# Layer scale on one core: held-back loads, 8-row first blocks, and stores released by a landing

## The chip, the cores and the metric

The kernel runs on one core of a Trainium2 chip. The metric is the device time in microseconds (us) of that core. It is a pure streaming job: two large inputs come in from device memory (HBM), one output of the same size goes out, and in between stand one multiplication and one addition for each element.

## The reference

```python
B, S, D = 1024, 16, 512
x: bfloat16 [B, S, D]
y: bfloat16 [B, S, D]
gamma: bfloat16 [D]

def reference(x, y, gamma):
    return x + gamma * y
```

Flattened, x and y have 16384 rows of 512 elements. The kernel gives each of the 128 partitions of on-chip memory (SBUF) 128 such rows. "A row" below means one row on every partition: 128 x 512 bf16 elements, 128 KB. x, y and the output have 128 of them each, so the DMA engines move 384 rows, 50.33 MB.

## The kernel before

Everything is laid out by a few tables at the head. `BLOCKS` cuts the 128 rows into blocks that are contiguous per partition in HBM; a DMA moves rows of one block, so a load of 64 rows moves 64 KB per partition in one packet. `PIECES` cuts the rows again for VectorE. `SP` lists the loads that SyncE issues, in order; `ACT` lists what ScalarE issues: gamma and the stores; `DVE` lists VectorE's multiplies ('m') and adds ('a') by piece.

```python
BLOCKS = [4, 64, 60]
PIECES = [4, 11, 53, 60]

SP = [
    ('y', 0, 4),
    ('y', 4, 68),
    ('x', 4, 68, 0),         # the last number: first slot in x_sb
    ('y', 68, 128),
    ('x', 68, 128, 11),
    ('x', 0, 4, 0),
]
ACT = [('g',), ('s', 4, 68), ('s', 68, 128), ('s', 0, 4)]

EARLY = (2, 0)               # SyncE's first two loads go before the start barrier

DVE = [('m', 0), ('m', 1), ('m', 2), ('a', 2), ('a', 1), ('m', 3), ('go',), ('a', 3), ('a', 0)]
```

y has its whole place in SBUF (128 slots of 1 KB per partition), and multiply and add work in place on it. x has 71 slots; its later blocks reuse the slots of the first block, so their loads wait until the adds that read those slots are done. Issuing, one list per engine (`_take` waits for a semaphore and takes its count off again):

```python
    def ring(eng, what, n_early):
        known, went = 0, False
        for k, w in enumerate(what):
            kind = w[0]
            need = frees(w) if kind == "x" else pieces_of(w[1], w[2]) + list(w[3:]) if kind == "s" else []
            need = max((order[c] + 1 for c in need), default=0)
            if kind == "s" and not went:
                _take(s_go, 1, eng)          # the first store waits for "go"
                went = True
            if need > known:
                eng.wait_ge(s_add, need)     # adds done so far
                known = need
            # ... dma_start of gamma, of an x load, of a y load, or of a store
```

gamma comes as one row, is spread over the 128 partitions by a matmul with a row of ones, and is cast to bf16:

```python
    nc.vector.memset(ones_row, 1.0).then_inc(s_ones, 1)
    _take(s_ones, 1, nc.tensor)
    _take(s_gamma, 16, nc.tensor)
    nc.tensor.matmul(gamma_ps, ones_row, gamma_row, start=True, stop=True).then_inc(s_ps, 1)
    _take(s_ps, 1, nc.vector)
    nc.vector.tensor_copy(out=gamma_sb, in_=gamma_ps).then_inc(s_dve, 1)
```

VectorE's list:

```python
    for kind, *args in DVE:
        if kind == "go":
            _take(s_dve, open_mults, nc.vector)   # all multiplies are done
            open_mults = 0
            nc.vector.sem_inc(s_go, 1)            # stores may start
            continue
        c = args[0]
        yt = y_sb[:, starts[c] : starts[c + 1], :]
        if kind == "m":
            need(y_loads, c)                      # waits for the y loads of this piece
            # ... yt = yt * gamma  (L166)
        else:
            need(x_loads, c)                      # waits for the x loads of this piece
            # ... yt = xt + yt     (L175)
```

Of the kernel before, what the change touches and what calls it, by code (L numbers as in the profile page):

```python
# [3 lines left out]

BLOCKS = [4, 64, 60]

PIECES = [4, 11, 53, 60]


SP = [
    ('y', 0, 4),
    ('y', 4, 68),
    ('x', 4, 68, 0),
    ('y', 68, 128),
    ('x', 68, 128, 11),
    ('x', 0, 4, 0),
]
ACT = [('g',), ('s', 4, 68), ('s', 68, 128), ('s', 0, 4)]  # L20

EARLY = (2, 0)

DVE = [('m', 0), ('m', 1), ('m', 2), ('a', 2), ('a', 1), ('m', 3), ('go',), ('a', 3), ('a', 0)]
MULT, ADD = mybir.AluOpType.mult, mybir.AluOpType.add


def _take(sem, n, eng):


    return eng.wait_ge(sem, n).then_inc(sem, -n)  # L31


def kernel(
    tc: tile.TileContext,
    x: bass.AP,
    y: bass.AP,
    gamma: bass.AP,
    out: bass.AP,
):  # L40

    nc = tc.nc
    P = nc.NUM_PARTITIONS
    tc.close()
    tc.compile()  # L47

    xf = x.flatten_outer_dims()
    yf = y.flatten_outer_dims()  # L50
    of = out.flatten_outer_dims()
    N, D = xf.shape
    rows = N // P
    n = len(PIECES)
    assert sum(PIECES) == rows
    starts = [sum(PIECES[:c]) for c in range(n + 1)]
    dt = xf.dtype
    edges = [sum(BLOCKS[:c]) for c in range(len(BLOCKS) + 1)]
    assert edges[-1] == rows

    def rows_of(t, a, b):

        c = max(c for c in range(len(BLOCKS)) if edges[c] <= a)
        assert b <= edges[c + 1]
        block = t[P * edges[c] : P * edges[c + 1]].rearrange("(p n) d -> p n d", p=P)
        return block[:, a - edges[c] : b - edges[c], :]

    gamma_row = nc.alloc_sbuf_tensor("gamma_row", [1, D], dt).ap()
    ones_row = nc.alloc_sbuf_tensor("ones_row", [1, P], dt).ap()
    gamma_sb = nc.alloc_sbuf_tensor("gamma_sb", [P, D], dt).ap()  # L70
    y_sb = nc.alloc_sbuf_tensor("y_sb", [P, rows, D], dt).ap()
    x_loads = [w for w in SP + ACT if w[0] == "x"]
    y_loads = [w for w in SP + ACT if w[0] == "y"]
    stores = [w for w in SP + ACT if w[0] == "s"]
    for loads in (x_loads, y_loads, stores):
        assert sum(w[2] - w[1] for w in loads) == rows
    x_rows = max(w[3] + w[2] - w[1] for w in x_loads)
    x_sb = nc.alloc_sbuf_tensor("x_sb", [P, x_rows, D], dt).ap()
    gamma_ps = nc.alloc_psum_tensor("gamma_ps", [P, D], mybir.dt.float32).ap()

    sem = nc.alloc_semaphore
    s_gamma, s_ones, s_ps, s_dve = sem("s_gamma"), sem("s_ones"), sem("s_ps"), sem("s_dve")
    s_load = {w: sem("s_" + "_".join(map(str, w[:2]))) for w in x_loads + y_loads}
    s_add, s_go, s_end, s_out = sem("s_add"), sem("s_go"), sem("s_end"), sem("s_out")
    added = [a for kind, *a in DVE if kind == "a"]
    order = {a[0]: k for k, a in enumerate(added)}

    def meets(a, b, c, d):
        return a < d and c < b

    def pieces_of(a, b):
        return [c for c in range(n) if meets(starts[c], starts[c + 1], a, b)]

    def x_at(row):
        return next(w[3] + row - w[1] for w in x_loads if w[1] <= row < w[2])

    def frees(w):

        c = set()
        for v in x_loads[: x_loads.index(w)]:  # L100
            lo, hi = max(v[3], w[3]), min(v[3] + v[2] - v[1], w[3] + w[2] - w[1])
            if lo < hi:
                c |= set(pieces_of(v[1] + lo - v[3], v[1] + hi - v[3]))
        return sorted(c)

    early = []

    def ring(eng, what, n_early):

        known, went = 0, False  # L110
        for k, w in enumerate(what):
            kind = w[0]
            need = frees(w) if kind == "x" else pieces_of(w[1], w[2]) + list(w[3:]) if kind == "s" else []
            need = max((order[c] + 1 for c in need), default=0)
            if kind == "s" and not went:
                _take(s_go, 1, eng)
                went = True
            if need > known:
                eng.wait_ge(s_add, need)
                known = need  # L120
            if kind == "g":
                i = eng.dma_start(out=gamma_row, in_=gamma.unsqueeze(0)).then_inc(s_gamma, 16)
            elif kind == "x":
                to = x_sb[:, w[3] : w[3] + w[2] - w[1], :]
                i = eng.dma_start(out=to, in_=rows_of(xf, w[1], w[2])).then_inc(s_load[w], 16)
            elif kind == "y":
                r = slice(w[1], w[2])
                i = eng.dma_start(out=y_sb[:, r, :], in_=rows_of(yf, w[1], w[2])).then_inc(s_load[w], 16)
            else:
                r = slice(w[1], w[2])  # L130
                i = eng.dma_start(out=rows_of(of, w[1], w[2]), in_=y_sb[:, r, :]).then_inc(s_out, 16)
            if k < n_early:
                early.append(i.ins)

    ring(nc.sync, SP, EARLY[0])
    ring(nc.scalar, ACT, EARLY[1])


    nc.vector.memset(ones_row, 1.0).then_inc(s_ones, 1)  # L139
    _take(s_ones, 1, nc.tensor)  # L140
    _take(s_gamma, 16, nc.tensor)
    nc.tensor.matmul(gamma_ps, ones_row, gamma_row, start=True, stop=True).then_inc(s_ps, 1)  # L142
    _take(s_ps, 1, nc.vector)
    nc.vector.tensor_copy(out=gamma_sb, in_=gamma_ps).then_inc(s_dve, 1)  # L144
    _take(s_dve, 1, nc.vector)

    landed, open_mults = set(), 0

    def need(loads, c):
        for w in loads:  # L150
            if w not in landed and meets(starts[c], starts[c + 1], w[1], w[2]):
                _take(s_load[w], 16, nc.vector)
                landed.add(w)

    for kind, *args in DVE:
        if kind == "go":
            _take(s_dve, open_mults, nc.vector)
            open_mults = 0
            nc.vector.sem_inc(s_go, 1)
            continue  # L160
        c = args[0]
        yt = y_sb[:, starts[c] : starts[c + 1], :]
        if kind == "m":
            need(y_loads, c)
            g = gamma_sb[:, None, :].to_broadcast([P, PIECES[c], D])
            nc.vector.tensor_tensor(out=yt, in0=yt, in1=g, op=MULT).then_inc(s_dve, 1)  # L166
            open_mults += 1
        else:
            need(x_loads, c)
            if open_mults:  # L170
                _take(s_dve, open_mults, nc.vector)
                open_mults = 0
            at = x_at(starts[c])
            xt = x_sb[:, at : at + PIECES[c], :]
            nc.vector.tensor_tensor(out=yt, in0=xt, in1=yt, op=ADD).then_inc(s_add, 1)  # L175


    nc.scalar.sem_inc(s_end, 1)
    _take(s_end, 1, nc.sync)
    _take(s_add, n, nc.sync)  # L180
    _take(s_out, 16 * len(stores), nc.sync)

    main = nc.main_func.blocks[0].instructions
    names = {i.name for i in early}
    for b in nc.main_func.blocks[1:]:
        for i in [i for i in b.instructions if i.name in names]:
            b.instructions.remove(i)
    for k, i in enumerate(early):
        main.insert(1 + k, i)
# [30 lines left out]
```

## Time and profile before

| what | before |
|---|---|
| device time, median of 3 runs | 120.48 us (120.41 to 120.82) |
| span of the profiled run (120.82 us) | 119.5 us |
| VectorE busy | 70.1 us (59%), 10 instructions |
| TensorE busy | 0.6 us (one matmul) |
| y rows 0 to 4: issued, landing | 0.0 us, 3.3 us later |
| first store issued | 76.98 us |
| first store (8 MB), issue to landing | 23.1 us |

How to read the profile: PE is TensorE, DVE is VectorE, POOL is GpSimd; SPq and ACTq are the sequencers of SyncE and ScalarE, which issue the DMAs. A line such as L166 is a line of the kernel. The span is cut into 40 slices, and each digit is the busy share of a slice in tenths. DMA is the mean busy share of the core's 16 DMA engines. A DMA queue is listed with its packets, its megabytes and the time that its packets took, as a share of 16 engines' span. A line of the timeline has the start, the time taken, the engine, the operation and its shapes; an "x2" joins two operations that follow each other. In brackets stands how long the engine had been idle before it.

### The profile page before, as it was taken

The numbers are of one execution on the slowest core, as the hardware profiler recorded it, in microseconds if no ns is written. First come the engines' busy times: TensorE is split into PE (matmuls) and PEld (weight loads), VectorE is DVE, ScalarE is ACT, GpSimd is POOL, SyncE is SP. The second block draws the span as 40 slices with busy tenths as digits, with TensorE's granted clock in tenths as the row PEclk, the third lists the DMA queues.
The fourth block names the chain that finished last, engine by engine and source line by source line (L and its number), as shares of the span: only waits on it lengthen the run. The fifth ranks groups of instructions, "written<-read, shape, count | busy, mean of one in ns | idle before, by whom it ended". The sixth has DMA issues, their size and how long they took to land. (4 is left out here: it accounts for less than half of the span.)

```text
span 119.5 us, 79 instructions
## 1 busy us (share of the span) xinstructions
PE 0.6 (0%) x1; PEld 0.1 (0%) x1; DVE 70.1 (59%) x10; POOL 0.2 (0%) x4
## 2 busy tenths in 40 slices
PE   0001000000000000000000000000000000000000
PEld 0000000000000000000000000000000000000000
DVE  0001400299999579999979999649999930000000
POOL 0000000000000000000000000000000000000000
DMA  9888998889888987987998998798998899899874
GB/s 527 351 351 351 483 570 351 351 351 702 351 351 351 639 370 329 617 370 329 535 432 350 411 555 350 329 527 351 592 439 373 351 557 432 350 473 494 350 337 167
DMA packets 1298, 50.33 MB, mean 421 GB/s; under 512 B 145, under 2 KB 146, under 8 KB 530
## 3 DMA queue, kind: packets, MB, share of 16 engines
q1 hardware_dynamic: 864, 33.55, 65.6%
q10 hardware_dynamic: 434, 16.78, 32.5%
HBM read 33.56 MB, written 16.78 MB: 421 GB/s over the span
## 5 line engine op out<-in xcount | busy, mean ns | idle before, releaser
L166 DVE TENSOR_TENSOR y_sb<-y_sb,gamma_sb 128x2048 bf16<-128x2048 bf16 (+3 forms) x4 | 34.7, 8690 | 10.5 <-DVEq L31 10.5
L175 DVE TENSOR_TENSOR y_sb<-x_sb,y_sb 128x27136 bf16<-128x27136 bf16 (+3 forms) x4 | 34.6, 8689 | 4.9 <-DVEq L31 4.9
L144 DVE CAST gamma_sb<-gamma_ps 128x512 bf16<-128x512 f32 x1 | 0.7, 692 | 9.3 <-DVEq L31 9.3
L139 DVE MEMSET ones_row<- 1x128 bf16 x1 | 0.2, 165 | 2.0 <-PEq L47 2.0
L142 PE MATMUL gamma_ps<-gamma_row,ones_row 1*128 1x512 bf16 x1 | 0.6, 577 | 10.7 <-PEq L31 10.7
L142 PEld LDWEIGHTS gamma_ps<-gamma_row,ones_row 1*128 1x128 bf16 x1 | 0.1, 99 | 10.7 <-issue 10.7
L204 POOL MEMSET const-bfloat16-1.0<- 128x1 bf16 x1 | 0.1, 102 | 0.0
L204 POOL MEMSET const-uint8-127<- 128x1 uint8 x1 | 0.1, 102 | 0.0
L204 POOL MEMSET const-float32-1.0<- 128x1 f32 x1 | 0.1, 99 | 0.0
L204 POOL MEMSET const-float32-0.0<- 128x1 f32 x1 | 0.1, 98 | 0.2 <-issue 0.2
## 6 DMA issues: line engine op xcount, KB each, us to landing
y_sb<-in_y_dram SPq DMA_DIRECT2D x1, 7680.0 KB, 58.1
x_sb<-in_x_dram SPq DMA_DIRECT2D x1, 7680.0 KB, 22.4
out_dram<-y_sb ACTq DMA_DIRECT2D x1, 7680.0 KB, 22.4
y_sb<-in_y_dram SPq DMA_DIRECT2D x1, 512.0 KB, 3.3
x_sb<-in_x_dram SPq DMA_DIRECT2D x1, 512.0 KB, 20.9
out_dram<-y_sb ACTq DMA_DIRECT2D x1, 512.0 KB, 22.7
y_sb<-in_y_dram SPq DMA_DIRECT2D x1, 22.5
x_sb<-in_x_dram SPq DMA_DIRECT2D x1, 40.4
```

Of the source, the lines that this page charges most:

```text
L139: nc.vector.memset(ones_row, 1.0).then_inc(s_ones, 1)
L142: nc.tensor.matmul(gamma_ps, ones_row, gamma_row, start=True, stop=True).then_inc(s_ps, 1)
L144: nc.vector.tensor_copy(out=gamma_sb, in_=gamma_ps).then_inc(s_dve, 1)
L166: nc.vector.tensor_tensor(out=yt, in0=yt, in1=g, op=MULT).then_inc(s_dve, 1)
L175: nc.vector.tensor_tensor(out=yt, in0=xt, in1=yt, op=ADD).then_inc(s_add, 1)
L204: nc = _bacc.Bacc("TRN2", target_bir_lowering=False, num_devices=1)
```

## The change

Three things change together.

- The blocks become 8, 60 and 60 rows in place of 4, 64 and 60, and VectorE's pieces 8, 15, 45 and 60 rows. x's 8 rows are its last load, and the last store has 8 rows. x now needs 75 slots.
- The third load (x), the fourth (y) and gamma are held back until y's first 8 rows have landed. TensorE waits for that landing and tells SyncE, ScalarE and VectorE by a semaphore each.
- The first store is no longer released by VectorE after the last multiply. TensorE waits until x's second block (rows 68 to 128) has landed, and then releases the stores and VectorE's last large add.

It is meant to keep the DMA queues short at the start, so that nothing goes beside the first rows, and to keep stores from running beside the last large load; x's 8 small rows are left in the queue to bridge the turn from loads to stores.

```diff
-BLOCKS = [4, 64, 60]
-PIECES = [4, 11, 53, 60]
+BLOCKS = [8, 60, 60]
+PIECES = [8, 15, 45, 60]

 SP = [
-    ('y', 0, 4),
-    ('y', 4, 68),
-    ('x', 4, 68, 0),
+    ('y', 0, 8),
+    ('y', 8, 68),
+    ('x', 8, 68, 0),
     ('y', 68, 128),
-    ('x', 68, 128, 11),
-    ('x', 0, 4, 0),
+    ('x', 68, 128, 15),
+    ('x', 0, 8, 0),
 ]
-ACT = [('g',), ('s', 4, 68), ('s', 68, 128), ('s', 0, 4)]
+ACT = [('g',), ('s', 8, 68), ('s', 68, 128), ('s', 0, 8)]

+HOLD = ('y', 0, 8)
+RELEASE = ('x', 68, 128, 15)
-DVE = [('m', 0), ('m', 1), ('m', 2), ('a', 2), ('a', 1), ('m', 3), ('go',), ('a', 3), ('a', 0)]
+DVE = [('m', 0), ('m', 1), ('m', 2), ('a', 2), ('a', 1), ('m', 3), ('a', 3), ('a', 0)]
 ... (semaphores s_held_sp, s_held_act, s_held_dve, s_rel)
         for k, w in enumerate(what):
             kind = w[0]
+            if k == n_early:
+                _take(s_held[eng], 1, eng)
 ...
     nc.vector.memset(ones_row, 1.0).then_inc(s_ones, 1)
+    _take(s_load[HOLD], 16, nc.tensor)
+    for s_one in s_held.values():
+        nc.tensor.sem_inc(s_one, 1)
     _take(s_ones, 1, nc.tensor)
     _take(s_gamma, 16, nc.tensor)
 ... (matmul and cast as before)
+    _take(s_load[RELEASE], 16, nc.tensor)
+    nc.tensor.sem_inc(s_go, 1)
+    nc.tensor.sem_inc(s_rel, 1)
 ... (VectorE's need())
-                _take(s_load[w], 16, nc.vector)
+                if w == RELEASE:
+                    _take(s_rel, 1, nc.vector)
+                elif w == HOLD:
+                    _take(s_held[nc.vector], 1, nc.vector)
+                else:
+                    _take(s_load[w], 16, nc.vector)
 ... (VectorE's list)
-        if kind == "go":
-            _take(s_dve, open_mults, nc.vector)
-            open_mults = 0
-            nc.vector.sem_inc(s_go, 1)
-            continue
```

## The prediction

> **What bounds the kernel now.** I read the page first (its slices, the DMA queues, the costliest groups), then VectorE's timeline, then tables of busy time by stage, then single packet records of the trace around the three places that the change touches: the start, the turn from loads to stores, and the end.
>
> The page's slices and its queue part come first:
>
> ```profile
> DVE  0001400299999579999979999649999930000000
> DMA  9888998889888987987998998798998899899874
> ...
> q1 hardware_dynamic: 864, 33.55, 65.6%
> q10 hardware_dynamic: 434, 16.78, 32.5%
> HBM read 33.56 MB, written 16.78 MB: 421 GB/s over the span
> ```
>
> The DMA engines are busy in every slice. The two queues' packets fill 65.6% + 32.5% = 98.1% of the 119.5 us, which is 117.2 us; so an average engine idles only 2.3 us, before its first packet and after its last. VectorE is busy for 59%. The loads are on q1 (SyncE's), the stores on q10 (ScalarE's).
>
> VectorE's timeline says what it waits for (start us, us, what; in brackets the idle time before):
>
> ```profile
> 12.36 1.23 DVE L166 TENSOR_TENSOR y_sb<-y_sb,gamma_sb 128x2048 bf16<-128x2048 bf16 x1 [0.26 <-DVEq L31]
> 23.06 17.29 DVE L166 TENSOR_TENSOR y_sb<-y_sb,gamma_sb 128x5632 bf16<-128x5632 bf16 x2 [9.48 <-DVEq L31]
> 42.52 17.29 DVE L175 TENSOR_TENSOR y_sb<-x_sb,y_sb 128x27136 bf16<-128x27136 bf16 x2 [2.16 <-DVEq L31]
> 60.55 16.16 DVE L166 TENSOR_TENSOR y_sb<-y_sb,gamma_sb 128x30720 bf16<-128x30720 bf16 x1 [0.74 <-DVEq L31]
> 79.41 17.30 DVE L175 TENSOR_TENSOR y_sb<-x_sb,y_sb 128x30720 bf16<-128x30720 bf16 x2 [2.70 <-DVEq L31]
> ```
>
> Every stage of VectorE starts when a load has landed and ends before the next one lands: it is 0.7 to 2.7 us ahead each time. Sixty rows cost it 16.16 us, the same rows cost the DMA 18.1 us (60 KB packets of 2.267 us, eight per engine and load). So VectorE sets no end; it only has to hand over the stores in time.
>
> The last view is busy time around the turn and at the end (in each row: stretch, its length, busy time of four engines, clock, DMA share, GB/s; a packet counts where it starts, so a share can pass 1):
>
> ```profile
> 77.70:80.41 2.71, 0.00 (x0) 0.00 (x0) 1.00 (x1) 0.00 (x0) 1.00 1.32 556
> 80.41:116.00 35.59, 0.00 (x0) 0.00 (x0) 16.30 (x2) 0.00 (x0) 1.00 0.99 429
> 116.00:119.50 3.50, 0.00 (x0) 0.00 (x0) 0.00 (x0) 0.00 (x0) 1.00 0.37 150
> ```
>
> From the first load to 116 us there is no hole. The packet records at the turn show why: VectorE's "go" at 76.7 us lets ScalarE issue the first store at 76.98; the fastest engine ends x's last 4 rows at 78.97 and starts its first store packet the same instant, the slowest does so at 80.41. At the end the 4 KB packets of the last store finish at 117.7 us on the fastest engine, at 118.5 on the last but one and at 119.1 on the last, whose completion is seen at 119.46. That last engine is late because one packet of x's rows 68 to 128, started at 59.71, took 3.30 us in place of 2.27.
>
> **What the Trainium skill says.** "DMA: Bandwidth & Descriptors", section "Issuing engines are not separate DMA queues": transfers issued by different engines run on the same 16 DMA engines. The trace agrees: the two queues' shares add up to 98.1%. The same page, section "Queues, rings and completion order", lets an engine go round-robin between its queues at packet boundaries. Here that is seen only in part: the slowest engine ended all eight packets of x's 4 rows before its first store packet at 80.41, though other engines were storing from 78.97. I therefore count on queued loads finishing first. "Perfetto Trace Analysis", section "DMA Instruction — HWDGE (DVE, Sync)": the reported time of a DMA instruction is its issue, and completion comes after a confirmed last write. The trace has 0.37 us for issuing the first store and 23.1 us to its landing. "VectorE: DVE Perf Modes", section "The perf-mode tier table", has bf16 tensor-tensor work at two elements a cycle, 1224 ns for 2048 elements; the trace has 1226 and 1220 ns.
>
> **The change part by part.**
>
> 1. Block sizes, 4/64/60 to 8/60/60. Bytes stay 384 rows of 128 KB. Per engine before: 24 packets of 64 KB at 2.418, 24 of 60 KB at 2.267 and 24 of 4 KB at 0.159 (medians of the trace): 58.03 + 54.41 + 3.82 = 116.26 us. After: 48 of 60 KB and 24 of 8 KB. The 8 KB packet I put on the line between 4 and 60 KB: 0.159 + 4 x 0.03764 = 0.310 us, an estimate. Sum 108.82 + 7.43 = 116.25 us. Difference: 0.0 us.
>
> 2. The hold at the start. y's first two loads, 68 rows, still go out at 0, as before. First packets start at 1.00; eight of 0.31 plus the slow start (about 0.46 us per engine over the median in the first load) end near 3.9 us, landing near 4.5. TensorE sees it and signals; SyncE issues the third load near 4.8 and the fourth near 5.2, in place of 1.90 and 2.28. The queue holds y's 60 rows until about 22.1, so these two come 17 us early still: cost 0. Gamma goes out near 4.8 in place of 1.91. It took until 10.65 before TensorE could use it, 8.7 us, mostly waiting behind two 2.4 us packets. The same 8.7 gives 13.5; TENSOR_TENSOR on 8 rows (4096/2/0.96 GHz plus the 0.16 us fixed term of the 2048-element one: 2.3 us) then runs from about 15.3 to 17.6. The next y rows land at 22.9. Cost 0, slack 5 us.
>
> 3. The middle. y's 60 rows land at 22.9 as before; multiplies for 15 + 45 rows take 16.2 us. x's first 60 rows land at 22.1 + 18.1 + 0.8 = 41.0; the 45-row add ends near 53.2, and only then is x's second block issued (56.84 before). Its engines get free near 59.2. Slack grows from 2.9 to about 6 us. x's 8 rows go out after the 15-row add, near 57.4 (59.8 before), behind the block: no hole.
>
> 4. The release. Before, the store was freed by VectorE's multiply, now by the landing of x's second block. The engines ended that block at 77.7 (fastest) to 78.6, and one at 79.2, the one held up. Landing plus TensorE's and ScalarE's hand-over I put at 0.3 us, and an issue needs 1.0 us (first load) to at most 2.0 (first store) to its first packet: 79.9 to 80.9 without a straggler. Meanwhile each engine has x's 8 rows, 8 x 0.31 = 2.5 us in place of 1.3: busy until 80.2 (fastest) to 81.1. At worst the fast engines idle 0.7 us; with a straggler ending at 79.2 they idle up to 1.3 us, but the straggler itself works until 81.7 and idles not at all. Since the end is the slowest engine's, this costs 0 to 0.2 us.
>
> 5. The end. The 60-row add can start near 78.6 instead of 79.41 and ends by 94.8; the second store is issued then, and the first store keeps the engines until about 98.5. 8 rows' add ends near 97.1, its store has until 116. Cost 0. The last packets are 8 KB and not 4 KB: 0.15 us more of the last write behind a landing at worst.
>
> Sum: 0.0 +- 0.2 us of work, plus what stragglers do. The profiled run was the slowest of three (120.82 against 120.41 and 120.48) and its last engine ended about 0.6 us after its neighbour. If the hold-up does not come back (both late issues, x's second block and x's small block, now lie clear of the moment at which the first ends its wait; before, the small block was issued at 59.8, within 0.1 us of the packet that took 3.30 us), 0.1 to 0.5 us go. I take a small gain of 0.2 us.
>
> **The rivals.** First, a hole at the turn: if a store needs the full 2 us to its first packet and the landing is late on all engines, all 16 would idle about 0.5 us, making 120.9 to 121.0. For it speaks that the release is now serial with the loads; against it, the 2.5 us of x rows queued behind. Second, the start gains: the third and fourth load and gamma were issued between 1.9 and 2.7 us, and the first 64 KB packets, started from 2.63 to 2.99, took 2.61 to 2.77 us on nine engines in place of 2.42. If these issues disturb running packets and the hold avoids it, 0.2 us would go: 120.2. Against it, the issues then fall at 5 us on other running packets. Third, VectorE becomes the bound if gamma waits for several more packets: it would need over 5 us more, so I give it little.
>
> **Range and chances.** 120.48 less 0.2 is 120.3 us. The three runs spread over 0.4 us, the hole can add 0.6 and the lost straggler take 0.5, so 119.9 to 120.9 should hold it eight times in ten. A 2% change needs 2.4 us, more than the whole idle time of an engine (2.3 us) on the fast side, and more than twice the hole I can construct on the slow side: 1% faster, 98% within, 1% slower.
>
> **What would show it.** The DMA shares should again sum to about 98%; gamma's matmul near 13.5; the 15-row multiply near 23; x's second block issued near 53; the first store issued near 78.5; the 60-row add starting within 0.3 us of that. Wrong would be: an idle stretch on all engines between 80 and 81.5; a store of rows 68 to 128 issued after 98; the 15-row multiply starting later than 23.5; or a busy time of the engines away from 117.2 us, which would mean that packet rates differ from those I have carried over.

## The result, and the profile after

The changed kernel takes 119.88 us (median of 6 runs, 119.75 to 119.96). The kernel before, run beside it, takes 120.56 us (6 runs, 120.30 to 120.82). The ratio is 0.9944, 95% interval 0.9928 to 0.9959: 0.7 us less, or 0.6%. That is within 2%, but three times the gain I had put down, and 0.02 us under the lower end of my range.

The page of the changed kernel, the same parts as before:

```profile
DVE  0000720199999399999499999569999950000000
...
DMA  5999799779779879879977977897997797797787
...
q1 hardware_dynamic: 864, 33.55, 65.8%
q10 hardware_dynamic: 434, 16.78, 32.7%
HBM read 33.56 MB, written 16.78 MB: 424 GB/s over the span
```

The queues' shares sum to 98.5% of 118.6 us (98.1% of 119.5 us before). Summed packet by packet, an engine works 116.9 us on average, and worked 117.1 us before. So its work fell by only 0.2 us, and its idle time from 2.4 to 1.7 us. The last DMA digit is what the reader should look at: 7 where it was 4. The engines now stop together.

The timeline of the changed kernel (start us, us, what):

```profile
5.23 0.33 SPq L132 DMA_DIRECT2D x_sb<-in_x_dram  x1
5.43 0.52 ACTq L129 DMA_DIRECT2D gamma_row<-in_gamma_dram  x1
...
13.24 2.29 DVE L180 TENSOR_TENSOR y_sb<-y_sb,gamma_sb 128x4096 bf16<-128x4096 bf16 x1 [0.26 <-DVEq L35]
23.17 16.23 DVE L180 TENSOR_TENSOR y_sb<-y_sb,gamma_sb 128x7680 bf16<-128x7680 bf16 x2 [7.63 <-DVEq L35]
41.42 16.23 DVE L189 TENSOR_TENSOR y_sb<-x_sb,y_sb 128x23040 bf16<-128x23040 bf16 x2 [2.02 <-DVEq L35]
53.60 4.40 SPq L132 DMA_DIRECT2D x_sb<-in_x_dram  x2
59.49 16.16 DVE L180 TENSOR_TENSOR y_sb<-y_sb,gamma_sb 128x30720 bf16<-128x30720 bf16 x1 [1.85 <-DVEq L35]
77.83 19.02 ACTq L138 DMA_DIRECT2D out_dram<-y_sb  x3
78.12 18.36 DVE L189 TENSOR_TENSOR y_sb<-x_sb,y_sb 128x30720 bf16<-128x30720 bf16 x2 [2.48 <-DVEq L35]
```

In the kernel before, the issue of x's last two loads stands at:

```profile
56.84 3.33 SPq L125 DMA_DIRECT2D x_sb<-in_x_dram  x2
```

In the first large block the changed kernel is not ahead: its 15-row multiply starts at 23.17, the old one's at 23.06, on the same 68 rows. The later stages start earlier largely because four rows fewer stand ahead of them. The last large add starts 1.3 us earlier (78.12 against 79.41). x's second block is complete 1.8 us earlier (77.48 against 79.28): 1.2 us are the four rows (60 rows take an engine 18.1 us), and the other 0.6 us come from the slowest engine. The way over TensorE takes 0.5 us of it back.

The same three stretches as before show the turn and the end:

```profile
77.70:80.41 2.71, 0.00 (x0) 0.00 (x0) 2.29 (x1) 0.00 (x0) 1.00 1.39 596
80.41:116.00 35.59, 0.00 (x0) 0.00 (x0) 16.07 (x2) 0.00 (x0) 1.00 0.97 422
116.00:119.50 3.50, 0.00 (x0) 0.00 (x0) 0.00 (x0) 0.00 (x0) 1.00 0.53 225
```

Where did the 0.9 us of these two spans go? The trace has one completion per engine and load. The 16 engines' last stores complete at 117.97 to 119.46 us before and at 118.23 to 118.61 after (the 118.01 of the first expectation below is the second of the 16). Their mean is 118.36 before and 118.41 after. **The average engine gained nothing; only the last one did.** The spread between the first and the last engine runs like this:

| completion of | before | after |
|---|---|---|
| y's first rows | 0.38 us | 0.38 us |
| y's first large block | 0.52 | 0.38 |
| y's second block | 0.53 | 0.38 |
| x's second block | 1.21 | 0.36 |
| last store | 1.49 | 0.38 |

The spread that arises at x's second block (1.21 us) is still there at the last store (1.49): in this kernel nothing evens it out, and what an engine loses at 60 us is still missing at 119. So the question for the experiments is what makes engines late at x's second block.

### The profile page after: what moved, and what is told of

It reads as the page before. It is cut to its first block, busy times and chain, and to the rows that moved or that the text cites. A ratio compares the mean times of both kernels' runs of the same rounds, so it can differ in the third digit from the quotient of the medians.

```text
span 118.6 us, 87 instructions
## 1 busy us (share of the span) xinstructions
PE 0.6 (0%) x1; PEld 0.1 (0%) x1; DVE 70.1 (59%) x10; POOL 0.2 (0%) x4
## 5 line engine op out<-in xcount | busy, mean ns | idle before, releaser
L180 DVE TENSOR_TENSOR y_sb<-y_sb,gamma_sb 128x4096 bf16<-128x4096 bf16 (+3 forms) x4 | 34.7, 8690 | 9.7 <-DVEq L35 9.7
L189 DVE TENSOR_TENSOR y_sb<-x_sb,y_sb 128x23040 bf16<-128x23040 bf16 (+3 forms) x4 | 34.6, 8688 | 4.5 <-DVEq L35 4.5
## 6 DMA issues: line engine op xcount, KB each, us to landing
out_dram<-y_sb ACTq DMA_DIRECT2D x1, 1024.0 KB, 22.1
```

## The experiments

Each edit is against the kernel named. Every run was timed beside the kernel before on the same chip; on these chips that kernel spreads from 119.8 to 122 us. The ratios use the runs within 1.5% of each kernel's fastest. "Lead" is the time from the issue of x's second block to the median start of its 16 first packets, in that run's profile. A packet of 60 KB that is not held up takes 2.267 to 2.29 us. The expectations letter their theories. Late engines come, by A, from the issue of x's small last load; by B, from the 64 KB packets or the block sizes; by C, from the loads queued at the start; by D, from an issue of x's second block that comes late; by E, from VectorE's adds beside the first packets; by I, from the block's place in SBUF. P and L refine D: by P only an issue just ahead of a packet step harms, by L a later one harms more.

### First round: is the late engine real, and which part of the change removes it?

**The kernel before once more**, with no edit.

> The kernel before, unchanged in what it does, to see whether its late engine is there in every run. In its first profile the 16 engines ended the last store 1.45 us apart (118.01 to 119.46), and the spread rose from 0.53 us (landing of y's rows 68 to 128) to 1.21 us (landing of x's rows 68 to 128); the changed kernel stays at 0.35 to 0.38 us throughout. If the late engine is a cause of the program, the spread jumps again at the same load, to over 0.9 us; if it was chance, it stays near 0.5 and the span is near 118.9. Time about 120.5 in both cases.

Measured: 120.82 us (22 runs, 120.01 to 122.06), ratio 0.9989 (0.9966 to 1.0012). Its profile fell on a quick run of 120.03 us, and there the spread at x's second block is only 0.46 us and no first packet is late. So the late engine is neither fixed nor a single chance. It comes in different sizes, and in the profiles the time follows it. Four profiled runs of kernels with the old blocks and a lead of 2.9 to 3.0 us show it:

| profiled run of | spread at x's second block | time of that run |
|---|---|---|
| e1 | 0.46 us | 120.03 us |
| e2 | 1.08 | 120.81 |
| before | 1.21 | 120.82 |
| e3 | 2.05 | 121.74 |

**Own slots for x's last 4 rows** (kernel before):

```diff
-    ('x', 0, 4, 0),
+    ('x', 0, 4, 71),
```

> Only x's first 4 rows get slots of their own, so their load is issued right after x's second block (near 57.2) and not at 59.8, where the engines begin on that block. Theory A, that an issue which falls on the first packets of another load holds engines up: the spread after x's second block stays near 0.5 us and the time falls by 0.5 to 0.7, to about 119.9. Theory B, that the late engine comes from 64 KB packets or from the block sizes, and theory C, that it comes from the loads queued at the start: no change, 120.5, spread over 0.9.

Measured: 120.85 us, ratio 0.9994 (0.9963 to 1.0025). The small load is now issued at 57.2 and two first packets still took 2.58 and 2.78 us. The engine with the longer one had also stood idle for 0.54 us just before it. Theory A, which the prediction had hinted at too, falls.

**The hold alone** (kernel before, `HOLD = ('y', 0, 4)` with its waits):

> Kernel before with the hold alone: third and fourth load and gamma are issued once y's first 4 rows have landed (near 3.7). Theory C (queueing at the start slows engines): spread of the first large landing falls from 0.52 to about 0.38, time falls by 0.2 to 0.7. Theories A and B: the spread still jumps at x's second block, time 120.4 to 120.6.

Measured: 120.99 us, ratio 1.0009 (0.9983 to 1.0036). First packets up to 2.96 us, and one engine idle for 0.98 us before its own. Theory C falls.

**The blocks alone** (changed kernel without hold and release):

```diff
-HOLD = ('y', 0, 8)
-RELEASE = ('x', 68, 128, 15)
+HOLD = None
+RELEASE = None
-DVE = [..., ('m', 3), ('a', 3), ('a', 0)]
+DVE = [..., ('m', 3), ('go',), ('a', 3), ('a', 0)]
```

> Block sizes 8, 60, 60 alone, with no hold, and the stores still released by VectorE. Theory B (sizes): time falls by 0.5 to 0.7 to about 119.9. Theory A: x's last 8 rows are issued near 57.5, before the engines begin on x's second block at about 58.7, so the collision is gone here too and the time falls alike: then this run tells C apart only, which expects 120.3 to 120.6.

Measured: 120.84 us, ratio 0.9996 (0.9971 to 1.0020), and none of the expected gain. But the runs are narrower (120.58 to 121.19), and in the profile x's second block has landed by 77.35 with a spread of 0.48 us: the late engine is gone. Something else takes the gain back behind it. The window from 75.5 to 79.3 of this kernel shows it, with that of the same blocks and the release (e6, below) second:

```profile
75.50:79.30 3.80, 0.00 (x0) 0.00 (x0) 1.81 (x1) 0.00 (x0) 1.00 0.67 205
```

```profile
75.50:79.30 3.80, 0.00 (x0) 0.00 (x0) 1.31 (x2) 0.00 (x0) 1.00 0.84 357
```

VectorE is done early and the store is issued at 75.75, while x's last block is still under way. The 8 KB packets of x's 8 rows then take 0.40 us in the mean and up to 0.70, in place of 0.309, with idle gaps between them of 0.2 us per engine. Eight packets that are 0.09 us longer make 0.76 us, so about 1 us in all, and the rows have landed at 80.75 in place of 79.96. The store gains nothing by its early issue: its first packet starts at 79.83, later than in the changed kernel (79.14), where it is issued at 77.83.

### Second round: release, hold, and a first test of the issue time

**The changed kernel again:**

> The changed kernel itself, on one chip with the next three and more often: its gain over the kernel before on this chip, and how far its runs spread. The kernel before ran from 119.9 to 121.8 in 59 runs, its late engines being there in some profiles (spread 1.4 to 2.3 us at the end) and absent in one (0.64). If the change removes late engines, its runs spread by under 0.4 us and its engines end within 0.4 us; if it only saves a constant, they spread as widely as before. Time 119.9, some 0.7 to 1.0 below the median of before.

Measured: 119.93 us (7 runs, 119.81 to 120.13), ratio 0.9919 (0.9889 to 0.9949). As narrow as expected in time; the end spread was 0.63 us, more than the 0.4 that I had expected, because four engines were 0.25 us ahead of the rest from the first block on.

**The changed kernel without the hold** (`HOLD = None`):

> The changed kernel without the hold: blocks 8, 60, 60 and the release by the landing. If the hold is idle weight: equal to the changed kernel within 0.2 us, 119.8 to 120.1. If the hold is what takes the late engines away: 120.3 or more, with a spread over 1 us. Compared with the blocks alone (120.84, stores issued at 75.75 while x's last rows were still coming, 8 KB packets then taking up to 0.70 in place of 0.31 us), the release alone should give 0.6 to 0.9 us if that meeting of stores and loads was the cost.

Measured: 119.95 us, ratio 0.9937 (0.9906 to 0.9968). The hold does nothing that shows in the time. Against the blocks alone the release is worth 0.9 us here (120.84 to 119.95; two chips, but both stand beside the same kernel before at 120.8 to 120.9).

**The release alone** (kernel before with `RELEASE = ('x', 68, 128, 11)`):

> Kernel before with the release alone, blocks still 4, 64, 60. x's 4 rows then bridge only 1.3 us, where landing, hand-over and first packet need 1.3 to 2.3: a hole of 0.3 to 1.0 us on the fast engines at about 79.5, and late engines as before. Expected 120.9 to 121.5, not faster than before. If it is faster than before by 0.4 or more, the release and not the block size carries the gain.

Measured: 121.12 us, ratio 1.0018 (0.9995 to 1.0040). As expected, no gain. The window around the turn, in the kernel before and then in this one:

```profile
76.50:80.50 4.00, 0.00 (x0) 0.00 (x0) 1.30 (x2) 0.00 (x0) 1.00 0.97 409
```

```profile
76.50:80.50 4.00, 0.00 (x0) 0.00 (x0) 0.95 (x2) 0.00 (x0) 1.00 0.74 310
```

The share falls from 0.97 to 0.74: the first store is issued at 79.57, its first packets start at 80.43, and engines that ended x's 4 rows at 79 wait for them: each of the 16 is idle for 0.4 to 1.6 us. This is the hole of my first rival. In the changed kernel the 8 rows fill it.

**A late issue in the changed kernel:**

```diff
-PIECES = [8, 15, 45, 60]
+PIECES = [8, 4, 56, 60]
-    ('x', 68, 128, 15),
+    ('x', 68, 128, 4),
```

> The changed kernel with pieces of 8, 4, 56 and 60 rows: the add that frees x's slots has 56 rows in place of 45, so x's second block is issued near 56.6, only 2.1 us before its first packets, as in the kernel before (56.8, 2.9 us ahead), and not at 53.6 (5 us). Theory D, that engines are held up when the next load's issue comes so late: late engines again at that load (packets over 2.5 us at about 58.7), ends spread by over 0.8 us, median 120.2 to 120.7. Theory B, that the 64 KB blocks are the cause: unchanged, 119.9 and a spread under 0.4.

Measured: 127.86 us in the median, 123.89 at best, for a reason that I had overlooked. With x's second block in slots 4 to 64, x's 8 rows in slots 0 to 8 must wait for that block's add:

```profile
77.96 45.02 ACTq L138 DMA_DIRECT2D out_dram<-y_sb  x3
78.25 16.16 DVE L196 TENSOR_TENSOR y_sb<-x_sb,y_sb 128x30720 bf16<-128x30720 bf16 x1 [2.72 <-DVEq L35]
94.44 0.33 SPq L132 DMA_DIRECT2D x_sb<-in_x_dram  x1
120.32 2.29 DVE L196 TENSOR_TENSOR y_sb<-x_sb,y_sb 128x4096 bf16<-128x4096 bf16 x1 [25.91 <-DVEq L35]
```

The load is issued at 94.44, queues beside the stores, and VectorE waits 25.9 us for it. The time of this run tells nothing of theory D; the next one repeats it without the mistake. Its first packets of x's second block ran before the mistake took effect: 2.2 us after the issue, 15 of them undisturbed and one of 2.44 us.

### Third round: issue time, VectorE, or block size

**The late issue, x's 8 rows in their own slots** (as e8, with `('x', 0, 8, 64)`):

> The late issue without the mistake of the run before it, in which x's last rows shared slots with x's second block and had to wait for its add (94.8). Changed kernel, pieces 8, 4, 56, 60, x's last 8 rows in slots of their own: x's second block is issued near 56.5, 2.1 to 2.5 us before its first packets; VectorE's adds still end near 57.6, before them. Theory D (a late issue holds engines up): late engines again, ends spread over 0.8 us, median 120.2 to 120.8. Theory E (VectorE at work when that block's first packets run: in the kernel before the adds end at 59.8, just on the first packets at 59.6 to 60.2) and theory B (64 KB packets): 119.9, spread under 0.4.

Measured: 120.02 us (11 runs, 119.86 to 120.51), ratio 0.9951 (0.9930 to 0.9972). Lead 2.3 us, and no late packet in the profile, which fell on the quickest run:

```profile
56.43 0.80 SPq L132 DMA_DIRECT2D x_sb<-in_x_dram  x2
```

A miss for theory D.

**The large blocks exchanged** (kernel before):

```diff
-BLOCKS = [4, 64, 60]
-PIECES = [4, 11, 53, 60]
+BLOCKS = [4, 60, 64]
+PIECES = [4, 11, 49, 64]
```

> Kernel before with its two large blocks exchanged: 4, 60, 64. The adds of 60 rows end near 57.3, more than 1 us before the first packets of x's second block (near 58.6 to 59); VectorE still releases the stores, at about 76.8 as in the kernel before. Theory E: no late engines, runs within 0.5 us of each other, median 119.9 to 120.1. Theory B: 64 KB packets are still half of all; as before, 120.8 and a spread of 1.5 us over the runs.

Measured: 120.28 us (20 runs, 119.91 to 120.77), ratio 0.9972 (0.9952 to 0.9992): between the two expectations. Lead 5.2 us; no first packet late in the profile, which fell on the quickest run. What costs most of its runs 0.3 us stays open.

**Blocks 8, 62, 58** (changed kernel, pieces 8, 15, 47, 58):

> Changed kernel with blocks 8, 62, 58. No 64 KB packets, and x's second block is issued near 54.6, 4.5 us ahead; but the adds of 62 rows end near 59.2, on the first packets of that block. Theory E: late engines come back, 120.2 to 120.8 and a wide spread. Theories B and D: 119.9 as the changed kernel.

Measured: 119.96 us (119.86 to 120.09), ratio 0.9942 (0.9922 to 0.9963). The adds end at 59.3, on the first packets. Five of these took 0.1 to 0.26 us over their 2.19 us (58 KB), although the lead is 4.0 us, but the time does not show it. So a small effect of the adds on packets is not excluded; as the cause of the lost time, theory E falls.

**Pieces 4, 15, 49, 60** (kernel before, nothing else):

```diff
-PIECES = [4, 11, 53, 60]
+PIECES = [4, 15, 49, 60]
-    ('x', 68, 128, 11),
+    ('x', 68, 128, 15),
```

> Kernel before with pieces 4, 15, 49, 60 (x's second block in slots 15 to 75): that block is issued near 55.7, 4 us before its first packets in place of 2.9; the adds still end at 59.8. Theory D: fewer late engines, median 120.0 to 120.4. Theories B and E: as before, 120.8.

Measured: 119.95 us (9 runs, 119.76 to 120.22), ratio 0.9944 (0.9920 to 0.9967). This edit alone, with blocks of 4, 64 and 60 rows, no hold and VectorE's go, gives a gain as large as the whole change. Its timeline:

```profile
42.34 17.29 DVE L196 TENSOR_TENSOR y_sb<-x_sb,y_sb 128x25088 bf16<-128x25088 bf16 x2 [2.17 <-DVEq L35]
55.59 4.40 SPq L132 DMA_DIRECT2D x_sb<-in_x_dram  x2
60.39 16.16 DVE L187 TENSOR_TENSOR y_sb<-y_sb,gamma_sb 128x30720 bf16<-128x30720 bf16 x1 [0.75 <-DVEq L35]
76.81 0.37 ACTq L138 DMA_DIRECT2D out_dram<-y_sb  x1
78.53 16.16 DVE L196 TENSOR_TENSOR y_sb<-x_sb,y_sb 128x30720 bf16<-128x30720 bf16 x1 [1.98 <-DVEq L35]
```

Up to 77 us VectorE's stages start as in the kernel before, to 0.2 us. What differs is that x's second block is issued at 55.59 in place of 56.84. It lands on the last engine at 78.4, not 79.3, and the last large add starts 0.9 us earlier. Theory B falls with it, since the 64 KB packets are still there.

### Fourth round: issue time or place in SBUF

e12 also moves the block's slots from 11 to 15. Three kernels take the two apart.

**Slot 15 at the old issue time** (kernel before, only `('x', 68, 128, 15)`):

> Kernel before, pieces as they were (issue of x's second block at 56.8), but that block in slots 15 to 75. Theory I (place in SBUF): median 119.9 to 120.1, runs within 0.5 us. Theory D (time of the issue): as before, 120.6 to 120.9, runs from 120 to 121.7.

Measured: 120.59 us (119.86 to 121.66), ratio 1.0004 (0.9974 to 1.0035): as the kernel before. The slot is not it.

**Slot 11 with an early issue** (changed kernel, pieces 8, 11, 49, 60):

> Changed kernel with pieces 8, 11, 49, 60 and x's second block in slots 11 to 71, issued near 54.7, 4 us ahead of its first packets. Theory I: late engines come back, median 120.3 or more, runs spread over 1 us. Theory D: 119.9 and narrow.

Measured: 119.93 us (16 runs, 119.79 to 120.08), ratio 0.9952 (0.9931 to 0.9972). Theory I falls.

**Pieces 4, 13, 51, 60** (kernel before):

> Kernel before with pieces 4, 13, 51, 60: issue near 56.2, slots 13 to 73. Theory D: the lead is 3.4 us, between 2.9 (wide) and 4.0 (narrow), so a median between 120.0 and 120.7 is expected, and some late engines. Theory I in the form that slot 11 alone is bad: 119.9 to 120.1.

Measured: 120.01 us (22 runs, 119.82 to 120.35), ratio 0.9946 (0.9929 to 0.9962). Half a microsecond more of lead (3.6 in place of 2.9 to 3.1 us) is enough.

### Fifth round: can the same be broken in the changed kernel?

**Pieces 8, 6, 54, 60**, x's 8 rows in slots of their own (66 to 74):

> Changed kernel, pieces 8, 6, 54, 60, x's last rows in slots of their own: x's second block issued near 55.9, 0.5 us before y's last packets start (56.4 in the median), as in the kernel before (56.8 against 57.4). Theory P (phase: descriptors that come in while the engines step to the last queued packet hold them up): late engines at about 58.7, median 120.2 or more, runs spread over 0.8 us. If the time in the changed kernel stays at 119.9 to 120.0 and narrow, phase is not it, and the cause is bound to the 64-row block or to VectorE's adds still running (until 59.8) beside such an issue.

Measured: 120.28 us (22 runs, 119.99 to 120.82), ratio 0.9979 (0.9958 to 0.9999). The late packets are back (10 of 16 over 2.32 us), with blocks of 8, 60 and 60, hold and release all in place:

```profile
55.91 0.80 SPq L132 DMA_DIRECT2D x_sb<-in_x_dram  x2
```

This is what theory P had expected; the next two runs test it further.

**Pieces 4, 7, 57, 60** (kernel before):

> Kernel before with pieces 4, 7, 57, 60: x's second block issued near 57.8, after y's last packets have started (57.3 to 57.8), and 1.8 us before its own first packets. Theory P: narrow again, 119.9 to 120.2. Theory L (in the kernel before the issue is simply too late, and later is worse): wide or wider, 120.7 to 121.5, with late packets at about 59.6, perhaps a hole.

Measured: 120.67 and 120.81 us, and four runs from 122.73 to 123.10 (no ratio is given for so wide a spread). No gain, and in the profile (of the run of 120.81) 6 of the 16 first packets took over 2.32 us, up to 2.66. Theory P, which wanted 119.9 to 120.2, fails.

**Pieces 8, 2, 58, 60**, x's 8 rows in slots of their own (62 to 70):

> Changed kernel, pieces 8, 2, 58, 60, x's last rows in slots of their own: x's second block issued near 57.0, after y's last packets have started (56.4) and 1.6 us before its own first packets, as far as in e17 (1.8). Theory L (the later the worse): late packets or a hole at about 58.7, median 120.7 to 123. Theory P (only an issue just ahead of a packet step harms): 119.9 to 120.2.

Measured: 120.65 us (22 runs, 120.37 to 120.84), ratio 0.9998 (0.9983 to 1.0014). The changed kernel's whole gain is gone, and theory P, which wanted 119.9 to 120.2, fails here too. The first packets of x's second block, in e14, e16 and e18, one line each; 819 GB/s over 1.2 us is all 16 packets of 60 KB, so share x 1.2 us is their mean duration:

```profile
58.20:59.40 1.20, 0.00 (x0) 0.00 (x0) 0.00 (x0) 0.00 (x0) 1.00 1.90 819
```

```profile
58.20:59.40 1.20, 0.00 (x0) 0.00 (x0) 0.00 (x0) 0.00 (x0) 1.00 2.00 819
```

```profile
58.20:59.40 1.20, 0.00 (x0) 0.00 (x0) 0.00 (x0) 0.00 (x0) 1.00 2.12 819
```

They give 2.28, 2.40 and 2.54 us (2.267, 2.396 and 2.541 from the packets themselves). In e18 the longest is 3.11 us, and 13 of 16 are over 2.32.

The kernels in which the issue time was moved or kept on purpose, by blocks and lead. Packets and idle time come from one profile of each, the medians from all runs. "Idle" is the longest time that one engine had nothing to do just before its first packet of x's second block:

| kernel | blocks | lead, us | longest first packet, us | idle, us | median, us |
|---|---|---|---|---|---|
| changed (e5) | 8, 60, 60 | 5.2 | 2.27 | 0.0 | 119.93 |
| e14 | 8, 60, 60 | 4.0 | 2.27 | 0.0 | 119.93 |
| e16 | 8, 60, 60 | 2.8 | 2.66 | 0.2 | 120.28 |
| e9 | 8, 60, 60 | 2.3 | 2.28 | 0.0 | 120.02 |
| e18 | 8, 60, 60 | 1.8 | 3.11 | 0.4 | 120.65 |
| e12 | 4, 64, 60 | 4.0 | 2.28 | 0.0 | 119.95 |
| e15 | 4, 64, 60 | 3.6 | 2.32 | 0.0 | 120.01 |
| before | 4, 64, 60 | 2.9 | 3.30 | 0.4 | 120.56 |
| e17 | 4, 64, 60 | 1.9 | 2.66 | 0.0 | 120.67 to 123.10 |

In this table no kernel with a lead of 3.6 us or more is harmed; below 3 us four of five are. (e10, not in it, is 0.3 us slower than the changed kernel with a lead of 5.2 us.) e9 is the exception, and it stays open: why a lead of 2.3 us did next to no harm there (and in the profile of e8, with the same issue time) while 2.8 and 1.8 did in the same blocks was not found. What inside the DMA engines holds a packet up when the issue comes late is open too. And in every one of these kernels the issue was moved by cutting VectorE's pieces differently; none delays the issue with the pieces unchanged, so that something else about the pieces takes part is not excluded. Nothing here went below the changed kernel: e12 and e14 equal it, e12 with far less of an edit.

## Why the prediction was wrong

**Part 1, the sizes: right.** The 8 KB packet took 0.309 us (0.310 estimated), the engines' work fell by 0.2 us with the late packets included, and e12, with the old sizes, is as fast as the changed kernel.

**Part 2, the hold: right in its worth, off in its times.** Cost 0 (e6). y's 8 rows landed at 4.9, not 4.5: eight engines began at 1.02 to 1.09 us with a packet of 0.97 to 1.30 us, the others only at 1.71 to 1.82. Gamma was usable at 11.57, not 13.5, so its wait was 6.1 us after its issue and not the 8.7 that I carried over. The 8-row multiply took 2.29 us (2.3). Neither landing nor gamma is on the path.

**Part 3, the middle: this step failed.** I had the time right (issue near 53.2, measured 53.60) and its meaning wrong. I wrote "slack grows from 2.9 to about 6 us" and "no hole", cost 0, taking any positive slack as free. It was not free: with a lead of 2.9 us some of the block's first packets took longer, by up to 1.04 us in the first profile, and the time is that of the slowest engine. I also read that profile as having no hole, and one engine had one: it stood idle for 0.37 us before its first packet, at 60.18. Moving this one issue by 1.25 us, with the pieces, brings as much as the whole change (e12); moving it back in the changed kernel takes more than half of the gain away in e16 (ratio 0.9979) and all of it in e18 (0.9998), though hardly any in e9 (0.9951). The new slack was mis-sized too: two blocks of 18.1 us after 22.1 us end at 58.3 and not at 59.2; the first packets started at 58.75, so the lead was 5.2 us and not 6.

**The sum: the right place, a wrong size.** I did see the packet of 3.30 us, did count the late engine as 0.6 us at the end, and did name the late issues as a possible cause. Then I booked it as chance: 0.1 to 0.5 us, taken as 0.2, where 0.68 us (0.49 to 0.87 by the interval) was measured. One profile and three runs could not tell an accident from a habit. The kernel before shows the late engine in one of its two profiles and runs from 119.8 to 122 us; the changed one shows it in neither of its two, and runs from 119.75 to 120.13. Of the two issues that I named, x's small block is innocent (e2), and the evidence points to x's second block.

**Part 4, the release: right in mechanism, unpriced in interplay.** There is no hole, thanks to the 8 rows (e7 shows it with 4), each engine did end its queued loads before its first store packet, and the first store went out at 77.83 where I had 78.5 or so. Two errors stand behind that. I kept the old ends of x's second block, although four rows fewer (1.2 us) stand ahead of it now; and even the old ones I had late: the packets ended at 77.72 to 78.40 and the late one at 78.88, not at 78.6 and 79.2. In the changed kernel they ended at 76.69 to 77.12. Landing and hand-over took 0.71 us, not 0.3. I missed what the new blocks would do without it: VectorE's go would come at 75.75 and cost 0.9 us (e4 against e6). The release alone is not a gain over the kernel before (e7); with the new blocks it keeps theirs.

**Part 5 and the rivals.** The end came as described, and the large add started at 78.12 (78.6). The hole did not appear in the changed kernel. The gain at the start did not appear: the first large block landed at 23.03 on its last engine, 0.1 us later than before. Gamma did not become the bound.

## What to carry to other kernels

In a kernel bound by DMA, look at the spread between the engines and not only at the queue's busy share: the span is set by the last engine, and what one engine loses early stays lost. A load that waits for a buffer should be issued well before the queue in front of it is used up; here 3.6 us was enough, 2.9 was not, and 2.3 was in one case. Cutting a smaller piece for the work that frees the buffer was the cheapest way to get there. Judge such a change by the spread of many runs, for a single profile of the same kernel had shown either 0.46 or 1.21 us.

## What was not expected of the hardware

- With a DMA issued 1.8 to 3 us before its first packets, these packets took up to 3.30 us in place of 2.27, on 2 to 13 of 16 engines, and in some profiles an engine stood idle before its own for up to 0.98 us (e3), though at the issue all engines still had packets to end. It is not constant from run to run: the profiles of e1 and e9 do not show it.
- A store issued at 75.75, with 4 us of loads still to come, did not start earlier than one issued at 77.83 (79.83 against 79.14), and the small load packets ahead of it took 0.40 us in place of 0.309.
- With a first load of 8 KB packets, half of the engines started 0.7 us after the others in the changed kernel, at 1.71 in place of 1.02 us (in e4 from 1.33 on); with the 4 KB packets of the kernel before all 16 started between 1.00 and 1.37.
